# Gated mix of linear and softmax attention: heads four at a time in quarter-array tiles, exponentials over three banks, and an order made by simulation

## The chip, the cores and the metric

One core of a Trainium2 chip. The time is that of one execution on the device, in microseconds (us), median of several; repeats of one kernel in its fast state agree within 0.8% for most kernels here and within 1.4% at the worst (two_banks). A run counts as slow when it is over 1.5% above the fastest of its kernel; times are compared between fast runs only. Engines as the profile names them: PE is the matmul engine (PEld its weight loads), ACT computes the exponentials, DVE does vector work, POOL more vector work, SP issues DMA. PSUM, into which PE writes, is laid out by both kernels as eight banks of 512 f32 values per partition.

Ratios are the mean time of one kernel's fast runs over the mean of the other's fast runs of the same rounds, so they are not quite the ratio of the medians quoted. The experiments ran on several chips; the kernel before took 1294 to 1300 us (medians) beside them, so where two experiments of different calls are compared I use their ratios to it.

## The reference, cut to what matters

```python
x = A_x                                             # 2048 x 512, bf16
g = sigmoid((x * gate_w).sum(-1, keepdims=True))
def A(x):   # linear attention, 32 heads of 16
    q, k, v = split_heads(x @ A_wqkv)
    pq, pk = q @ w_phi[h], k @ w_phi[h]             # 16x16 per head
    phi = lambda p: concat(softmax(p), softmax(-p)) # 32 features
    o = (phi(pq) @ (phi(pk).T @ v)) / (phi(pq) @ phi(pk).sum(seq) + 1e-6)
    return merge_heads(o) @ A_wo
def B(x):   # softmax attention, 32 heads of 16
    q, k, v = split_heads(x @ B_wqkv)
    return merge_heads(softmax(q @ k.T / 4) @ v) @ B_wo
out = g * A(x) + (1 - g) * B(x)
```

Branch B has 32 x 2048 x 2048 exponentials, a million per partition. They set a floor for ACT. PE must deliver the scores in time, with a contraction of only 16 rows (the projections contract over 128).

## The kernel before

All operations carry a guessed time stamp; each engine's instructions are sorted by it and issued in that fixed order. A unit of branch B is two heads, 512 queries and 128 keys: two score matmuls of 64 rows (the other heads' rows of q are zero), one exponential over two banks, two value matmuls.

```python
def add_qk(u, ts_):                       # L436
    for hf in range(2):
        p0 = 64 * hf
        ins = e.matmul(sT[b][:, NQ * hf:NQ * (hf + 1)], lhsT=kT_B[p0:p0 + 64, r, 128 * kt:128 * (kt + 1)],
                       rhs=q64[p0:p0 + 64, m, :], start=True, stop=True, tile_position=(p0, 0))
def add_exp(u, ts_):                      # L447: 128x1024; waits for the value matmuls of three units before
    exp_ops[u] = sch.add("act", ts_, lambda e: e.activation(E_B[:, eb, :], sT[b], ACTF.Exp, scale=SCALE), ...)
def add_pv(u, ts_):                       # L463: 32 columns per head, into one of two accumulators psO
    ...
def add_norm(blk, ts_):                   # 64 blocks of 16 units
    # L480 reciprocal of the whole 64x512 accumulator, L484 clamp,
    # L492 matmul that broadcasts the denominators, L503 copy, L507 product
    op_r = sch.add("dve", tk(t0, 0), lambda e: e.reciprocal(Rb32[p0:p0 + 64, :], psO[par][p0:p0 + 64, :]), ...)
    ...
```

Before the first unit, all k, v and q of branch B (first quarter of queries) are projected. Branch A is threaded between the units; its feature map is a chain PE, DVE (four operations), ACT, DVE (two), POOL.

The softmax here doesn't subtract the row's maximum and nothing guards it: scores larger than these inputs give would overflow.

Of the kernel before, what the change touches and what calls it, by code (L numbers as in the profile page):

```python
# [11 lines left out]

D = 512
H = 32
DH = 16
KT = D // 128
NQ = 512
HP = H // 2
VW = 17
VAW = H * VW + 16  # L20
SCALE = 1.0 / math.sqrt(DH)
SPACING_K = 9.0
SPACING_Q = 45.0
PROJ_STEP = 2.0
EVAC_DELAY = 1.0
STAT_DELAY = 2.0
EPS_TS = 1e-6


class _Op:  # L30
    __slots__ = ("ts", "order", "eng", "fn", "sem", "inc", "waits", "count", "name")

    def __init__(self, ts, order, eng, fn, sem, inc, waits, name):
        self.ts = ts
        self.order = order
        self.eng = eng
        self.fn = fn
        self.sem = sem
        self.inc = inc
        self.waits = waits  # L40
        self.count = None
        self.name = name


class _Sched:
    ENGINES = ("sp", "act", "pe", "dve", "pool")

    def __init__(self):
        self.ops = []
        self.n = 0  # L50
        self.sem_engine = {}

    def add(self, eng, ts, fn, sem=None, waits=(), inc=1, name=""):
        assert eng in self.ENGINES
        ws = []
        for w in waits:
            if w is None:
                continue
            assert isinstance(w, _Op), w
            assert w.ts < ts + 2.5, f"wait on future op: {name}@{ts} waits {w.name}@{w.ts}"  # L60
            assert w.sem is not None, f"producer {w.name} has no semaphore"
            if w.ts >= ts:
                ts = w.ts + EPS_TS
            ws.append(w)
        if sem is not None:
            key = id(sem)
            if key in self.sem_engine:
                assert self.sem_engine[key] == eng, "semaphore incremented by two engines"
            else:
                self.sem_engine[key] = eng  # L70
        op = _Op(ts, self.n, eng, fn, sem, inc, ws, name)
        self.n += 1
        self.ops.append(op)
        return op

    def emit(self, block):
        per_eng = {e: [] for e in self.ENGINES}
        for op in self.ops:
            per_eng[op.eng].append(op)
        for e in self.ENGINES:  # L80
            per_eng[e].sort(key=lambda o: (o.ts, o.order))
        totals = {}
        for e in self.ENGINES:
            for op in per_eng[e]:
                if op.sem is not None:
                    k = id(op.sem)
                    totals[k] = totals.get(k, 0) + op.inc
                    op.count = totals[k]
        starters = {
            "sp": block.sync,  # L90
            "act": block.scalar,
            "pe": block.tensor,
            "dve": block.vector,
            "pool": block.gpsimd,
        }
        for e in self.ENGINES:
            ops = per_eng[e]
            if not ops:
                continue

            def body(engine, ops=ops):
                waited = {}
                for op in ops:
                    for w in op.waits:
                        k = id(w.sem)
                        if waited.get(k, -1) >= w.count:
                            continue
                        engine.wait_ge(w.sem, w.count)
                        waited[k] = w.count
                    ins = op.fn(engine)  # L110
                    if op.sem is not None:
                        assert ins is not None, op.name
                        ins.then_inc(op.sem, op.inc)

            starters[e](body)
# [18 lines left out]
def _build(ctx, nc, A_x, A_wqkv, A_w_phi, A_wo, B_wqkv, B_wo, gate_w, out):  # L134
    S = A_x.shape[1]
    assert A_x.shape[2] == D and S % NQ == 0
    NT = S // 128
    NTQ = NQ // 128
    QC = S // NQ
    KTL = S // 128  # L140
    U = QC * HP * KTL
    TB = 40.0
    _cnt = [0]

    def sb(shape, dt=BF16):
        _cnt[0] += 1
        return ctx.enter_context(nc.sbuf_tensor(f"sbt{_cnt[0]}", shape, dt))

    def tk(base, n):
        return base + n * EPS_TS  # L150

    xT = sb([128, KT, S])
    W_A = sb([128, KT, 3 * D])
    W_B = sb([128, KT, 3 * D])
    Wq64 = sb([128, KT, 16, 128])
    WoA = sb([128, KT, D])
    WoP = sb([128, 8, D])
    Wbd = sb([128, KT, 128])
    kqT_A = sb([128, KT, S])
    vAz = sb([128, NT, 8, 72])  # L160
    kT_B = sb([128, KT, S])

    def ga_ap(i):
        return vAz[:, i, :, :].rearrange("p g c -> p (g c)")[:, 0:D]
    q64 = sb([128, 16, NQ])
    vaug = sb([128, KTL, VAW])
    phi_k = sb([128, 2, 1024])
    phi_q = sb([128, 2, 1024])
    _wbflat = W_B[:].rearrange("p t c -> p (t c)")
    DA = _wbflat[:, 0:2048].rearrange("p (b f) -> p b f", b=2)  # L170
    EA = _wbflat[:, 2048:4096].rearrange("p (b f) -> p b f", b=2)
    statA = sb([128, 2, 3, 64], F32)
    mtmp = sb([128, 3, 64], F32)
    kv_sb = sb([128, 8, 65], F32)
    kzbd = sb([128, 8, 68])
    mask64 = sb([128, 64])
    mask4 = sb([128, 4])
    E_B = sb([128, 3, 1024])
    oTn = sb([128, 2, 8, NQ])
    Rb = sb([128, NQ])  # L180
    Rb32 = sb([128, NQ], F32)
    bcs = sb([128, NQ])
    phi_qT = sb([128, 2, 8, 128])
    oA = sb([128, 2, D])
    oAT = sb([128, 2, KT, 128])
    ident = sb([128, 128])
    sel = sb([128, 64])
    ones = sb([128, 1])
    gw = sb([128, KT])
    g_sb = sb([128, NT], F32)  # L190
    omg = sb([128, NT], F32)
    eg = sb([128, NT], F32)
    fin = sb([128, 2, D])
    denr = sb([128, 2, 32], F32)

    psA = ctx.enter_context(nc.psum_tensor("psA", [128, 2048], F32))
    psO = [ctx.enter_context(nc.psum_tensor(f"psO{i}", [128, 512], F32)) for i in range(2)]
    psM6 = ctx.enter_context(nc.psum_tensor("psM6", [128, 512], F32))
    psM7 = ctx.enter_context(nc.psum_tensor("psM7", [128, 512], F32))
# [3 lines left out]
    s_x = sem("s_x")  # L203
    s_wA = sem("s_wA")
    s_wop = sem("s_wop")
    s_woA = sem("s_woA")
    s_wact = sem("s_wact")
    s_gw = sem("s_gw")
    s_wbd = sem("s_wbd")
    s_out = [sem(f"s_out{i}") for i in range(NT)]  # L210
    s_qk = sem("s_qk")
    s_pv = sem("s_pv")
    s_pe = sem("s_pe")
    s_act = sem("s_act")
    s_dve = sem("s_dve")
    s_pool = sem("s_pool")

    sch = _Sched()
    tasks = []

    def task(ts_, fn):
        tasks.append((ts_, len(tasks), fn))

    op_x = None
    for t in range(KT):
        op_x = sch.add("sp", tk(0.0, t),
                       lambda e, t=t: e.dma_start_transpose(xT[:, t, :], A_x[0, :, t * 128:(t + 1) * 128]),  # L227
                       sem=s_x, inc=16, name=f"dmaxT{t}")
    op_wB = sch.add("act", 0.0, lambda e: e.dma_start(W_B[:], B_wqkv.rearrange("(t p) c -> p t c", p=128)),
                    sem=s_wact, inc=16, name="dmaWB")  # L230
    op_wA = sch.add("sp", 0.1, lambda e: e.dma_start(W_A[:], A_wqkv.rearrange("(t p) c -> p t c", p=128)),
                    sem=s_wA, inc=16, name="dmaWA")
    gwv = gate_w.rearrange("(t p o) -> t p o", p=128, o=1)
    for t in range(KT):
        op_gw = sch.add("pool", tk(0.0, t), lambda e, t=t: e.dma_start(gw[:, t:t + 1], gwv[t]),
                        sem=s_gw, inc=16, name=f"dmagw{t}")

    op_id0 = sch.add("pool", 0.1, lambda e: e.iota(ident[:], [[-1, 128]], channel_multiplier=1,
                                                   allow_small_or_imprecise_dtypes=True), sem=s_pool, name="iota_id")
    op_ident = sch.add("pool", 0.2, lambda e: e.tensor_single_scalar(ident[:], ident[:], 0.0, ALU.is_equal),  # L240
                       sem=s_pool, waits=[op_id0], name="ident")
    op_ones = sch.add("pool", 0.21, lambda e: e.memset(ones[:], 1.0), sem=s_pool, name="ones")
    m64tmp = mtmp[:, 0, :]
    m64tmp2 = mtmp[:, 1, :]
    op_m1 = sch.add("pool", 0.3, lambda e: e.iota(m64tmp.rearrange("p (g c) -> p g c", c=16), [[-32, 4], [0, 16]],
# [49 lines left out]
    for t in range(KT):  # L295
        for j in range(8):
# [5 lines left out]
            op_wbd.append(o)  # L302
    op_wbd_done = op_wbd[-1]

    class Slot:
        def __init__(self, ap):
            self.ap = ap
            self.last_readers = []
# [588 lines left out]
```

## Time and profile before

| | kernel before |
|---|---|
| time, three runs | 1295.46 us (1291.0 to 1299.47) |
| first exponential of branch B | 64.3 us |
| exponentials at their shortest period, added up | 955.0 us |
| everything beyond that between first and last of them | 254.8 us |
| from the start of the last one to the end | 22.1 us |

An exponential's *free period* is the shortest distance from its start to the next one's that repeats: 0.904 us for 128x1024 out of PSUM (0.945 us for the feature maps' 128x1024 out of SBUF). What an interval has above it is called **stall** below. This is better than the mean duration in the profile's groups, which reaches into the next instruction.

The page of the kernel before: busy time, three rows of the forty slices, and costly groups (busy us, mean ns of one, then idle time before them and its releaser).

```profile
PE 1029.4 (79%) x5568; PEld 307.2 (24%) x5568; DVE 639.6 (49%) x773; ACT 995.3 (77%) x1058; POOL 111.1 (9%) x92
...
PE   4999876767698888869687888776878887877775
...
ACT  0077686787777899867698987986989799988993
...
PEclk9989887797889999889799989998999979988998
...
L447 ACT ACTIVATE sbt<-psA 128x1024 bf16<-128x1024 f32 x1024 | 967.6, 1061 | 208.2 <-PE psA L436 205.0
...
L480 DVE RECIPROCAL sbt<-psO 64x512 f32<-64x512 f32 x64 | 214.7, 3355 | 278.7 <-PE psO L463 278.7
```

No engine is full. ACT does the obligatory work and waits 208 us, nearly all for score matmuls (L436). Its first two slices are empty.

Timeline before, in a stretch where PE keeps up (start us, length us, what, idle time before it and its releaser):

```profile
1232.11 0.39 PE L436 MATMUL psA<-sbt 64*128 64x512 bf16 x2 [0.20 <-ACT sbt L447]
...
1232.43 0.39 PE L463 MATMUL psO<-sbt 128*32 128x512 bf16 x2
...
1233.03 0.39 PE L436 MATMUL psA<-sbt 64*128 64x512 bf16 x2 [0.20 <-ACT sbt L447]
...
1233.97 0.40 PE L492 MATMUL psM<-sbt 64*64 64x512 bf16 x1 [0.56 <-DVE sbt L484]
...
1234.30 0.39 PE L463 MATMUL psO<-sbt 128*32 128x512 bf16 x2
```

A score pair starts every 0.92 us, and its value pair follows 0.32 us later: the two matmuls of a pair overlap. The last two lines are the trouble: PE stands before the broadcast matmul L492, which waits for the reciprocal and the clamp, and the value pair behind it in PE's order starts 1.27 us after its score pair in place of 0.32.

### The profile page before, as it was taken

The numbers are of one execution on the slowest core, as the hardware profiler recorded it, in microseconds if no ns is written. First come the engines' busy times: TensorE is split into PE (matmuls) and PEld (weight loads), VectorE is DVE, ScalarE is ACT, GpSimd is POOL, SyncE is SP. The second block draws the span as 40 slices with busy tenths as digits, with TensorE's granted clock in tenths as the row PEclk, the third lists the DMA queues.
The fourth block names the chain that finished last, engine by engine and source line by source line (L and its number), as shares of the span: only waits on it lengthen the run. The fifth ranks groups of instructions, "written<-read, shape, count | busy, mean of one in ns | idle before, by whom it ended". The sixth has DMA issues, their size and how long they took to land.

```text
span 1296.3 us, 14382 instructions
## 1 busy us (share of the span) xinstructions
PE 1029.4 (79%) x5568; PEld 307.2 (24%) x5568; DVE 639.6 (49%) x773; ACT 995.3 (77%) x1058; POOL 111.1 (9%) x92
## 2 busy tenths in 40 slices
PE   4999876767698888869687888776878887877775
PEld 1422221222222222212122222221222222222221
DVE  2734566676655455443544545435445455444332
ACT  0077686787777899867698987986989799988993
POOL 9500011111100000000000000000000000000000
PEclk9989887797889999889799989998999979988998
DMA  6100000000000000000000000000000000000000
GB/s 162 34 1 1 1 1 1 1 1 1 1 1 1 1 1 1 1 1 17 1 1 1 1 1 13 5 1 1 1 1 1 17 1 1 1 1 1 1 1 17
DMA packets 14069, 9.34 MB, mean 7 GB/s; under 512 B 9904, under 2 KB 12976, under 8 KB 14000
## 3 DMA queue, kind: packets, MB, share of 16 engines
q1 hardware_dynamic: 12320, 6.82, 1.9%
q10 hardware_dynamic: 528, 1.57, 0.4%
q8 instruction: 44, 0.72, 0.2%
q14 instruction: 25, 0.20, 0.0%
q0 software_dynamic: 1152, 0.02, 0.0%
HBM read 4.21 MB, written 2.10 MB: 5 GB/s over the span
## 4 chain that ended last, share of the span: by engine, by line
issue 50%; PE 26%; DVE 11%; ACT 8%; POOL 3%; SPq 1%; DMA 0%; ACTq 0%; POOLq 0%; DVEq 0%
PE psA L436 8%; DVE sbt L480 8%; ACT sbt L447 7%; PE psO L463 7%; PE psM L322 6%; POOL sbt L641 3%; PE psA L322 2%; PE psM L523 1%; DVE sbt L484 1%; PE psM L492 1%; SPq L227 1%; PE psM L801 0%; DMA sbt<-in_A_x_dram 0%; PE psM L722 0%; DVE sbt L628 0%
## 5 line engine op out<-in xcount | busy, mean ns | idle before, releaser
L447 ACT ACTIVATE sbt<-psA 128x1024 bf16<-128x1024 f32 x1024 | 967.6, 1061 | 208.2 <-PE psA L436 205.0
L436 PE MATMUL psA<-sbt 64*128 64x512 bf16 x2048 | 426.6, 413 | 124.9 <-ACT sbt L447 115.7
L463 PE MATMUL psO<-sbt 128*32 128x512 bf16 x2048 | 427.6, 414 | 0.7 <-ACT sbt L447 0.7
L480 DVE RECIPROCAL sbt<-psO 64x512 f32<-64x512 f32 x64 | 214.7, 3355 | 278.7 <-PE psO L463 278.7
L436 PEld LDWEIGHTS psA<-sbt 64*128 64x128 bf16 x2048 | 99.2, 94 | 434.5 <-ACT sbt L447 321.8
L322 PE MATMUL psM<-sbt 128*128 128x512 bf16 x448 | 138.0, 441 | 74.1 <-DVE sbt L610 33.5
L463 PEld LDWEIGHTS psO<-sbt 128*32 128x32 bf16 x2048 | 99.5, 94 | 259.3 <-issue 257.8
L641 POOL TENSOR_TENSOR sbt<-sbt 128x1024 bf16<-128x1024 bf16 x32 | 61.7, 1929 | 1078.0 <-DVE sbt L633 1029.9
L326 DVE CAST sbt<-psM 128x512 bf16<-128x512 f32 x90 | 61.8, 687 | 93.9 <-PE psM L322 93.5
L322 PEld LDWEIGHTS psM<-sbt 128*128 128x128 bf16 x448 | 39.5, 105 | 139.0 <-issue 90.8
L503 DVE CAST sbt<-psM 64x512 bf16<-64x512 f32 x64 | 44.0, 687 | 33.2 <-PE psM L492 32.7
L383 ACT ACTIVATE sbt<-psM 128x16 f32<-128x16 f32 x1 | 0.2, 184 | 61.5 <-PE psM L378 61.5
L628 DVE TENSOR_REDUCE sbt<-sbt 128x64 f32<-128x1024 bf16 x32 | 38.8, 1212 | 16.6 <-ACT sbt L619 16.3
L507 DVE TENSOR_TENSOR sbt<-psO,sbt 64x512 bf16<-64x512 f32 x64 | 44.1, 689 | 2.2
L322 PE MATMUL psA<-sbt 128*128 128x512 bf16 x128 | 30.9, 397 | 17.8 <-DMA sbt<-in_A_x_dram 17.8
L492 PE MATMUL psM<-sbt 64*64 64x512 bf16 x64 | 29.1, 455 | 18.3 <-DVE sbt L484 13.3
L619 ACT ACTIVATE sbt<-sbt 128x1024 bf16<-128x1024 bf16 x32 | 35.0, 1095 | 9.1 <-DVE sbt L610 9.1
L598 DVE TENSOR_REDUCE sbt<-psM 128x32 f32<-128x512 f32 x32 | 22.0, 686 | 36.6 <-PE psM L588 30.2
L523 PE MATMUL psM<-sbt 128*128 128x512 bf16 x128 | 31.8, 394 | 4.5 <-DVE sbt L531 3.0
L728 DVE COPY sbt<-psM 128x1024 bf16<-128x1024 bf16 x16 | 11.0, 686 | 35.5 <-PE psM L722 35.3
L531 DVE SCALAR_TENSOR_TENSOR sbt<-psM,sbt 128x512 bf16<-128x512 f32 x16 | 12.0, 750 | 32.5 <-PE psM L523 32.5
L484 DVE TENSOR_SCALAR sbt<-sbt 64x512 bf16<-64x512 f32 x64 | 26.9, 421 | 2.1
(65 smaller groups left out, 365.6 us busy)
## 6 DMA issues: line engine op xcount, KB each, us to landing
out_dram<-sbt SPq DMA_DIRECT2D x16, 128.0 KB, 1.7
sbt<-in_B_wqkv_dram ACTq DMA_DIRECT2D x1, 1536.0 KB, 8.8
sbt<-in_A_wqkv_dram SPq DMA_DIRECT2D x1, 1536.0 KB, 7.6
sbt<-in_B_wo_dram SPq DMA_DIRECT2D x8, 64.0 KB, 2.9
sbt<-in_A_w_phi_dram POOLq DMA_DIRECT2D x32, 0.5 KB, 1.8
sbt<-in_A_wo_dram SPq DMA_DIRECT2D x1, 512.0 KB, 4.3
sbt<-in_A_x_dram SPq DMA_TRANSPOSE x4, 7.6
sbt<-in_gate_w_dram POOLq DMA_DIRECT2D x4, 0.2 KB, 7.4
```

The source lines that it names most:

```text
L322: ins = e.matmul(slot.ap, lhsT=lhsT_list[i], rhs=rhs_list[i], start=(i == 0), stop=(i == n - 1))
L326: evac_fn = lambda e, slot=slot, dst_ap=dst_ap: e.tensor_copy(dst_ap, slot.ap)
L436: ins = e.matmul(sT[b][:, NQ * hf:NQ * (hf + 1)], lhsT=kT_B[p0:p0 + 64, r, 128 * kt:128 * (kt + 1)], rhs=q64[p0:p0 + 64, m, :], start=True ...
L447: exp_ops[u] = sch.add("act", ts_, lambda e: e.activation(E_B[:, eb, :], sT[b], ACTF.Exp, scale=SCALE), sem=s_act, waits=waits, name=f"exp ...
L463: ins = e.matmul(psO[par][c0:c0 + 32, :], lhsT=vaug[:, kt, VW * h: VW * h + 32], rhs=E_B[:, eb, NQ * jb: NQ * (jb + 1)], start=(kt == 0), ...
L480: op_r = sch.add("dve", tk(t0, 0), lambda e: e.reciprocal(Rb32[p0:p0 + 64, :], psO[par][p0:p0 + 64, :]), sem=s_dve, waits=w, name=f"recip{ ...
L484: lambda e: e.tensor_scalar(Rb[p0:p0 + 64, :], Rb32[p0:p0 + 64, :], 1e30, -1e30, op0=ALU.min, op1=ALU.max),
L492: lambda e: e.matmul(psM7[p0:p0 + 64, :], lhsT=sel[p0:p0 + 64, :], rhs=Rb[p0:p0 + 64, :], start=True, stop=True, tile_position=(p0, p0)),
L503: op_cp = sch.add("dve", tk(t0, 1), lambda e: e.tensor_copy(bcs[p0:p0 + 64, :], psM7[p0:p0 + 64, :]), sem=s_dve, waits=wcp, name=f"bccp{blk}")
L507: lambda e: e.tensor_tensor(dst, psO[par][p0:p0 + 64, :], bcs[p0:p0 + 64, :], ALU.mult),
L523: ins = e.matmul(psM7[:], lhsT=oTn[:, qc % 2, j, 128 * i:128 * (i + 1)], rhs=WoP[:, j, :], start=(j == 0), stop=(j == 7))
L641: lambda e: e.tensor_tensor(phi_dst[:, buf, :].rearrange("p (g f) -> p g f", f=DH), EA[:, buf, :].rearrange("p (g f) -> p g f", f=DH), rs. ...
```

## The change

The kernel is rewritten. Its intent:

- q is masked so that a head needs 32 rows; four heads sit in four 32-row tiles of the array. Score tiles are cut in threes, so that an exponential covers three banks (the first 32 still two). Query projections fall from 256 matmuls to 64.
- The accumulator of four heads is copied out by a DVE block transpose, after which the denominators are 16 values per partition: the reciprocal is small, and no broadcast matmul is needed.
- w_phi is multiplied into the projection weights once; gate and 1/denominator are folded together.
- Projections ("fills") are issued one matmul at a time between score and value groups.
- The order comes from a simulation with a duration for each operation; eight exponential buffers replace three.

The diff, cut to its core (the comments are mine; `...` marks cuts):

```diff
-        exp_ops[u] = sch.add("act", ts_, lambda e: e.activation(E_B[:, eb, :], sT[b], ACTF.Exp, scale=SCALE), ...
+        n = 2 if s < 64 else min(3, NTILE - s)
...
+                ins = e.matmul(psS[:, 512 * (base + m):512 * (base + m + 1)],
+                               lhsT=kT_B[32 * i:32 * i + 32, hg // 2, 128 * kt:128 * (kt + 1)],
+                               rhs=qz[32 * i:32 * i + 32, qc % 2, hg, :], start=True, stop=True,
+                               tile_position=(32 * i, 0))
+        op = P.add("pe", 0.30, -100, fn, reads=reads, writes=[("S", j % 2)], name=f"qk{j}")
...
+        op = P.add("act", 0.07 + 0.000833 * 512 * n, 0.0, lambda e: e.activation(
+            Ebuf[:, j % ERING, 0:512 * n], psS[:, 512 * base:512 * (base + n)], ACTF.Exp, scale=SCALE), ...
...
-            op_r = sch.add("dve", tk(t0, 0), lambda e: e.reciprocal(Rb32[p0:p0 + 64, :], psO[par][p0:p0 + 64, :]),
+        P.add("dve", 0.69, -50, lambda e: e.transpose(Tf[:, bb, :], psO[:]), reads=["psO"], ...
+        P.add("dve", 0.15, -40, lambda e: e.reciprocal(rd[:, bb, :], tv[:, :, DH]), reads=[("Tf", bb)], ...
...
+    MM = 0.216                      # simulated duration of one fill matmul
+    def fill(prio, mms, reads, banks=None, name="", chunk=1, dur=MM, after=()):
...
+LAT = 0.12                          # simulated time from one engine's end to another's start,
+MARGIN = 0.35                       # and more where DVE or POOL answers PE or ACT
```

## The prediction

> **What bounds the kernel now.** Span 1296.3 us. The page's busy list gives PE 1029 us (79%), ACT 995 (77%), DVE 640. Neither big engine is full, so I read stages.
> - Up to 63 us (slices, timeline) ACT does nothing: all of k, v, q of the attention branch is projected first; x lands only at 17.8 us.
> - From 63 to 1275 us ACT runs 1024 exponentials of 128x1024. Where PE keeps up (timeline, 500 to 504 and 1230 to 1234 us) one starts every 0.917 us: 939 us, plus 32 feature-map exponentials, about 30 us. The rest is ACT idle: 208 us, 205 of it put down to score matmuls (groups, waits), which stand in PE's fixed order behind a 3.36 us reciprocal (64 of them, 215 us of DVE), projections and feature maps; from 170 to 320 us ACT is at 75% and the granted clock 0.81 to 0.83.
> - Tail: the last exponential is about 21 us before the end.
>
> **What the change does.**
> - Scores come from four 32-row tiles; an exponential covers three banks: 661 of 128x1536, 32 of 128x1024. From 0.917 = 1024 x 0.833 ns + 64 ns I estimate 1.344 us for 1536. The Trainium skill ("ScalarE: Activation LUTs", What ACT_TABLE_LOAD costs) gives 0.833 ns per element plus a fixed part; the period agrees. ACT: 661 x 1.344 + 32 x 0.917 + 32 = about 950 us, only 20 less. The main gain is the 208 us of waiting and 50 us of start.
> - PE: a score pair takes 0.31 to 0.33 us, a value pair the same (timeline, 1234 to 1236 us: 0.645 per unit). Three tiles at once should cost about 0.7 us per 1.344 ("TensorE: Matmul & The Clock Gate", Measured speedup: three column tiles 2.38x; the trace shows only pairs). 694 x 0.7 = 486 us, plus about 180 for 530 full projections and small ones: 670 of 950. Query projections fall from 256 to 64 matmuls.
> - DVE: reciprocals, clamps, casts, products (330 us) become 32 block transposes and small work (50 us); DVE about 290. POOL takes two subtractions per feature map, about 130 us in all.
> - Order: a simulated schedule with eight exponential buffers replaces guessed times, so PE should seldom be stuck before a score matmul.
>
> **Critical path after.** ACT from first to last exponential. First at about 13 us (first quarter of x at 9, projection, copy). Stalls 18 us: 8 in the first head group, which has 84 projection matmuls beside 32 units, 10 around feature maps (whose exponential waits for POOL) and block boundaries. Tail about 9 us: value matmul, transposes, output matmul, store. 13 + 950 + 18 + 9 = **990 us**, range 963 to 1028. Faster by over 2%: 0.97; within 2%: 0.02; slower: 0.01.
>
> **What would show it.** ACT over 93% busy, digits 9 from the second slice; the three-bank exponential at a period near 1.344 us; ACT idle before it under 40 us; PE at most 75%; DVE near 300 us; the chain mostly ACT; first exponential before 15 us.
>
> **What would make it wrong.** Three 32-row tiles not overlapping (score group over 0.6 us): PE bounds, 1100 us or more. PE's granted clock falling to half because PE is less busy, so that the order runs late. ACT stuck behind feature-map exponentials whose POOL inputs are slower than the order assumed (1 us each adds 32). The 24 transposing loads landing later than 9 us.

## The result, and the profile after

| | before | after |
|---|---|---|
| time | 1294.16 us (1291.0 to 1299.47, 4 runs) | 1018.69 us (1017.72 to 1021.52, 4 runs) |
| first exponential of branch B | 64.3 us | 17.4 us |
| free periods added up | 955.0 us | 938.6 us |
| stall | 254.8 us | 49.2 us |
| last one's start to the end | 22.1 us | 10.8 us |
| profiled span | 1296.3 us | 1015.9 us |

The ratio is 0.7867 (95% interval 0.7842 to 0.7892). Of the 280 us between the two profiles, 206 are stall, 47 start, 16 shorter work and 11 tail.

The same parts of the page after:

```profile
PE 864.9 (85%) x5118; PEld 210.8 (21%) x5118; DVE 309.8 (30%) x595; ACT 958.5 (94%) x729; POOL 141.8 (14%) x131
...
PE   7988888878798788788889888888889888888986
...
ACT  3889999998989989999999999999999999999996
...
PEclk8999999997968868955557655555556655555765
...
L512 ACT ACTIVATE E_t<-psS 128x1536 bf16<-128x1536 f32 (+2 forms) x694 | 934.5, 1675 | 33.0 <-PE psS L500 26.4
...
L548 DVE STREAM_TRANSPOSE Tf_t<-psO 128x512 f32<-128x512 f32 x32 | 22.8, 713 | 400.7 <-PE psO L530 400.7
```

ACT is full as predicted, and DVE fell to 310 us. One row was not predicted: the granted PE clock. It is near full up to about 200 us, uneven up to 430 us, and then half of full speed with few exceptions. PE's busy share **rose** to 85% although it does less. By stretch, from the windows view (us, then busy time and instruction count of PE, PEld, DVE, ACT and POOL, then the granted clock, DMA share and GB/s):

```profile
60.00:200.00 140.00, 119.67 (x861) 35.74 (x860) 92.97 (x150) 139.40 (x109) 61.67 (x47) 1.00 0.00 1
200.00:480.00 280.00, 232.54 (x1601) 70.38 (x1598) 148.04 (x308) 261.51 (x197) 66.50 (x50) 0.77 0.01 3
480.00:980.00 500.00, 437.96 (x2292) 85.28 (x2289) 44.85 (x96) 493.50 (x367) 0.00 (x0) 0.55 0.01 3
```

Timeline after, once at full and once at half clock:

```profile
152.15 0.39 PE L500 MATMUL psS<-qz_t,kTB_t 32*128 32x512 bf16 x3
...
152.47 0.40 PE L530 MATMUL psO<-E_t,vaug_t 128*32 128x512 bf16 x3
...
640.59 0.61 PE L500 MATMUL psS<-qz_t,kTB_t 32*128 32x512 bf16 x3 [0.19 <-ACT E_t L512]
...
641.13 0.61 PE L530 MATMUL psO<-E_t,vaug_t 128*32 128x512 bf16 x3
...
641.94 0.61 PE L500 MATMUL psS<-qz_t,kTB_t 32*128 32x512 bf16 x3 [0.19 <-ACT E_t L512]
```

At full clock a value group starts 0.32 us after its score group, as before, although there are now three matmuls in each: quarter tiles do overlap. At half clock it is 0.54 us. Two groups then take 1.08 us of an exponential's 1.344 us, and 0.26 us are left for fills.

The stall by stretch, from the same intervals: 9.1 us up to 100 us, 0.2 us from 100 to 200, 25.6 us from 200 to 450 (branch A's query side), 14.3 us from 450 to the end. The last part comes in lumps, at about 480, 546, 780 and 955 us, while fills (a q projection, then the output projections) run. In between, at half clock, ACT loses nothing to speak of.

### The profile page after: what moved, and what is told of

It reads as the page before. It is cut to its first block, busy times and chain, and to the rows that moved or that the text cites. A ratio compares the mean times of both kernels' runs of the same rounds, so it can differ in the third digit from the quotient of the medians.

```text
span 1015.9 us, 11834 instructions
## 1 busy us (share of the span) xinstructions
PE 864.9 (85%) x5118; PEld 210.8 (21%) x5118; DVE 309.8 (30%) x595; ACT 958.5 (94%) x729; POOL 141.8 (14%) x131
## 4 chain that ended last, share of the span: by engine, by line
ACT 71%; PE 17%; DVE 9%; DMA 1%; issue 1%; SPq 0%; POOL 0%; DVEq 0%
ACT E_t L512 69%; PE psM L435 6%; PE psS L500 4%; PE psO L530 3%; ACT EA_t L670 2%; PE psS L435 1%; DVE oA_t L737 1%; PE psM L712 1%; DVE denr_t L730 1%; DVE stat_t L674 1%; PE psM L719 1%; DVE Pf_t L655 1%; DMA xT_t<-in_A_x_dram 1%; PE psM L739 1%; DVE denr_t L728 1%
## 5 line engine op out<-in xcount | busy, mean ns | idle before, releaser
L512 ACT ACTIVATE E_t<-psS 128x1536 bf16<-128x1536 f32 (+2 forms) x694 | 934.5, 1675 | 33.0 <-PE psS L500 26.4
L500 PE MATMUL psS<-qz_t,kTB_t 32*128 32x512 bf16 x2048 | 363.5, 521 | 98.8 <-ACT E_t L512 95.4
L530 PE MATMUL psO<-E_t,vaug_t 128*32 128x512 bf16 x2048 | 366.7, 526 | 1.2 <-DVE Tf_t L548 0.8
L500 PEld LDWEIGHTS psS<-qz_t,kTB_t 32*128 32x128 bf16 x2048 | 70.8, 96 | 397.3 <-ACT E_t L512 348.4
L530 PEld LDWEIGHTS psO<-E_t,vaug_t 128*32 128x32 bf16 x2048 | 71.3, 99 | 245.2 <-issue 230.8
L435 PE MATMUL psM<-Wp_t,xT_t 128*128 128x512 bf16 x128 | 38.4, 406 | 4.0 <-DVE phiQT_t L715 1.0
L674 DVE TENSOR_REDUCE stat_t<-EA_t 128x64 f32<-128x1024 bf16 x32 | 38.6, 1207 | 5.2 <-ACT EA_t L670 5.0
L435 PE MATMUL psM<-xT_t,WB_t 128*128 128x512 bf16 x112 | 34.6, 418 | 5.7 <-DVE qz_t L464 2.2
L670 ACT ACTIVATE EA_t<-Dd_t 128x1024 bf16<-128x1024 bf16 x32 | 38.4, 1201 | 0.0
L659 DVE TENSOR_REDUCE stat_t<-Pf_t 128x32 f32<-128x512 f32 x32 | 21.7, 679 | 0.9
L661 DVE TENSOR_REDUCE stat_t<-Pf_t 128x32 f32<-128x512 f32 x32 | 21.4, 670 | 0.0
L719 PE MATMUL psM<-kzbd_t,phiQT_t 128*128 128x68 bf16 x128 | 10.9, 216 | 10.9 <-DVE oA_t L737 9.9
```

What stands on the lines that cost most here:

```text
L435: return [lambda e, ap, i=i: e.matmul(ap, lhsT=lhs[i], rhs=rhs[i], start=(i == 0), stop=(i == len(lhs) - 1)) for i in range(len(lhs))]
L500: ins = e.matmul(psS[:, 512 * (base + m):512 * (base + m + 1)], lhsT=kT_B[32 * i:32 * i + 32, hg // 2, 128 * kt:128 * (kt + 1)], rhs=qz[32 ...
L512: op = P.add("act", 0.07 + 0.000833 * 512 * n, 0.0, lambda e: e.activation(Ebuf[:, j % ERING, 0:512 * n], psS[:, 512 * base:512 * (base + ...
L530: ins = e.matmul(psO[32 * i:32 * i + 32, :], lhsT=vaug[:, kt, VW * h:VW * h + 32], rhs=Ebuf[:, j % ERING, 512 * m:512 * (m + 1)], start=(k ...
L670: ex = P.add("act", 0.93, -4, lambda e: e.activation(EA[:, b, :], Dd[:, b, :], ACTF.Exp), reads=[("D", b, 0), ("D", b, 1)], writes=[("EA", ...
L674: P.add("dve", 1.22, prio, lambda e: e.tensor_reduce(stat[:, b, 1, :], e3, AX.X, ALU.add), reads=[("EA", b)], writes=[("ss", b)], name=f"s ...
```

## The experiments

The questions were: is the clock the cause of the remaining stalls (theory A), or does PE stand in its fixed order behind late answers of DVE (theory B); why is the clock low; and what did each part of the change buy?

| run | time, us | ratio | first exponential | stall | tail |
|---|---|---|---|---|---|
| the change | 1018.7 | 0.787 | 17.4 | 49.2 | 10.8 |
| before_copy | 1179.6 | 0.907 | 64.4 | 132.1 | 21.5 |
| before_32rows | 1448.8 | 1.115 | 65.6 | 403.6 | 24.3 |
| two_banks | 1205.3 | 0.928 | 16.2 | 213.9 | 10.9 |
| full_recip | 1030.5 | 0.792 | 16.6 | 60.4 | 14.0 |
| whole_fills | 1037.4 | 0.799 | 18.0 | 69.8 | 10.7 |
| keep_warm | 1012.5 | 0.778 | (slow profile) | | |
| keep_warm_again | 1008.9 | 0.775 | (slow profile) | | |
| start_tail | 1023.3 | 0.788 | 12.7 | 60.4 | 9.4 |
| start_tail_margin | 999.8 | 0.771 | 13.2 | 34.9 | 9.5 |
| margin | 1005.4 | 0.774 | 17.0 | 37.3 | 10.7 |
| late_plain | 995.5 | 0.766 | 13.4 | 39.2 | 9.8 |
| late_junk | 999.7 | 0.771 | 13.2 | 38.7 | 9.7 |

Times are medians of four runs each (for keep_warm the 2091 us run among them); the ratio is to the kernel before. First exponential, stall and tail are of the profiled run.

### before_copy: what the reciprocal cost the kernel before

```diff
-  e.reciprocal(Rb32[p0:p0 + 64, :], psO[par][p0:p0 + 64, :])
+  e.tensor_copy(Rb32[p0:p0 + 64, :], psO[par][p0:p0 + 64, :])
```

> The kernel before, with its 3.36 us reciprocal replaced by a copy of the same shape (0.69 us); wrong result on purpose. Theory: the normalization chain holds the score matmuls of PE in most of the 64 blocks (about 2 us each), so 100 to 150 us of the 242 us of waiting for scores go: 1150 to 1200 us. Rival: the waiting comes from projections and feature maps in PE's order; then at most 40 us go: 1255 us or more.

Measured: 1179.57 us, ratio 0.9068; the result is wrong, as intended. The stall fell from 254.8 to 132.1 us. The waits of ACT in the kernel before and then in this one:

```profile
ACT sbt L447 <- PE psA L436: 205.0, 166, 7.2
```

```profile
ACT sbt L447 <- PE psA L436: 96.1, 140, 6.0
```

The theory's range held (1150 to 1200 us): the length of the reciprocal alone accounted for about half of the waiting of the kernel before. The granted clock rose with it, from 0.91 to 0.95 or more, so a part of the gain may have come by way of the clock. The other half of the waiting is left when that chain is short; it was not split further (the prediction put it down to projections and feature maps in PE's order).

### full_recip: the slow reciprocal put back into the changed kernel

```diff
+        P.add("dve", 3.36, -40, lambda e: e.reciprocal(Tr[:], Tf[:, bb, :]), reads=[("Tf", bb)], writes=["Tr"], ...)
-        P.add("dve", 0.15, -40, lambda e: e.reciprocal(rd[:, bb, :], tv[:, :, DH]), ...)
+        P.add("dve", 0.15, -40, lambda e: e.tensor_copy(rd[:, bb, :], Tr[:].rearrange(...)[:, :, DH]), ...)
-ERING = 8
+ERING = 7
```

> The changed kernel with the full 128x512 reciprocal (3.36 us) back in each of the 32 blocks, after the block transpose has freed the bank (seven exponential buffers in place of eight, for room). Theory: once the accumulator is copied out by the transpose, a slow reciprocal is off the path: plus 3.4 us at the end and 0 to 5 us elsewhere, 1020 to 1030 us. Rival: VectorE being held for 3.4 us delays the drains of PE's fills, and 32 blocks lose 2 us each: about 1080 us.

Measured: 1030.52 us, ratio 0.7921 against 0.7867. This is at the slow edge of the theory's range (1020 to 1030 us) and far from its rival's 1080. The tail grew by 3.2 us, as it must; the stall by 11 us, of which 6.3 us came between 100 and 200 us, where DVE is busy with feature maps; how much of that is the missing eighth buffer and how much DVE being held is not told apart. So the transpose that frees the accumulator first is what took the reciprocal off the path: a reciprocal of the same 3.36 us, 32 times, costs 7 us (by the ratios) to 12 us (by the medians) here, where its 64 copies had cost the old structure about 120.

### two_banks: exponentials over two banks throughout

```diff
-        n = 2 if s < 64 else min(3, NTILE - s)
+        n = 2
```

> The changed kernel with every exponential over two banks (1024 of 128x1024). Theory: ScalarE bounds, so only its fixed part counts: 1024 x 0.917 against 661 x 1.344 + 32 x 0.917 is plus 21 us, that is about 1040 us, with the granted clock higher because PE does the same work per shorter period. Rival: at half clock a score and a value group take 1.08 us, more than 0.917, so that PE bounds wherever the clock is low: 1060 to 1120 us, ScalarE idle over 80 us.

Measured: 1205.28 us, ratio 0.9278. The rival was right, and by more than it said: 187 us slower, not 21. The page of this kernel, then its timeline:

```profile
PE 1157.2 (97%) x5077; PEld 270.8 (23%) x5118; DVE 300.3 (25%) x595; ACT 1054.4 (88%) x1059; POOL 141.9 (12%) x131
...
PEclk9999999689997555555555555555555555555555
...
```

```profile
699.86 0.60 PE L500 MATMUL psS<-qz_t,kTB_t 32*128 32x512 bf16 x2
...
700.39 0.61 PE L530 MATMUL psO<-E_t,vaug_t 128*32 128x512 bf16 x2
...
700.94 0.60 PE L500 MATMUL psS<-qz_t,kTB_t 32*128 32x512 bf16 x2
```

A score and a value group take 1.08 us at half clock whether they hold two tiles or three. Against 0.904 us of ACT that makes PE the bound; against 1.330 us it does not. The third bank pays because it puts half as much exponential work again behind the same PE time, far more than because of the 16 us of fixed cost that it saves ACT.

### before_32rows: one size changed in the kernel before

```diff
-  lhsT=kT_B[p0:p0 + 64, r, 128 * kt:128 * (kt + 1)], rhs=q64[p0:p0 + 64, m, :]
+  lhsT=kT_B[p0:p0 + 32, r, 128 * kt:128 * (kt + 1)], rhs=q64[p0:p0 + 32, m, :]
```

> The kernel before, its score matmuls contracting over 32 rows of the array in place of 64; everything else, order and counts included, is the same (wrong result on purpose: half of the heads are left out). Theory: the granted clock follows how much of the array the matmuls use, and not how busy PE is; so the clock, 0.91 before, falls to about 0.5 in the stretches without projections, groups take 0.54 us each, a unit 1.08 us, and the time rises by 60 to 150 us. Rival: the low clock of the changed kernel comes from PE being idle more of the time (long periods, fewer fills); then clock and time stay at 0.91 and 1300 us.

Measured: 1448.81 us, ratio 1.115; every instruction, its order and its waits are those of the kernel before. (The comparison with the reference still passed, though half of the heads' rows were left out. So it does not see an error in the scores of this size.) The windows of the kernel before, then of this one:

```profile
475.00:945.00 470.00, 377.94 (x2057) 110.11 (x2057) 218.76 (x261) 387.05 (x414) 17.09 (x10) 0.92 0.01 3
1096.00:1282.00 186.00, 141.70 (x784) 39.57 (x782) 78.34 (x84) 164.09 (x176) 3.85 (x2) 0.92 0.00 1
```

```profile
475.00:945.00 470.00, 428.24 (x1834) 106.13 (x1833) 194.45 (x232) 359.88 (x367) 15.41 (x8) 0.65 0.01 3
1096.00:1282.00 186.00, 175.51 (x750) 43.15 (x748) 80.58 (x97) 149.54 (x153) 7.71 (x4) 0.62 0.01 3
```

Half as many rows per score matmul, nothing else in the program, and the granted clock falls from 0.92 to 0.62, while PE is busy for more of the time (its matmuls take longer at the lower clock). So the clock did not fall because PE was idle. (The data change with the rows: the heads left out now give scores of zero. That this moved the clock is not excluded here, but in the changed kernel no head is left out, and its clock is low too.) In the changed kernel PE never stood idle for more than 0.63 us between 480 and 1005 us, at a clock of about 0.55; in the kernel before it stood idle for up to 3.4 us between 1096 and 1279 us and kept 0.92. In these runs what counts is how much of the array a matmul uses; by which measure exactly, they do not say.

The Trainium skill ("TensorE: Matmul & The Clock Gate", What's actually happening) says that the clock is set "based on how busy the PE has been recently", and its section "Why this matters for your kernels" advises against PE-idle gaps of over about 3 us. The two levels that it gives, half and full, agree with the clock records of these traces, which hold only 0.5 and 1.0; a granted clock between them is a mean over time. The advice about gaps does not suffice: PE with no gap above 0.63 us, in narrow tiles, was held at half for most of the time.

### keep_warm and keep_warm_again: buying the clock back

```diff
+            for _ in range(junk):        # 1 from the 141st score group on
+                e.matmul(psS[:, 512 * base:512 * base + 512], lhsT=kT_B[:, 0, 0:128], rhs=kT_B[:, 0, 0:512],
+                         start=True, stop=True)
-        op = P.add("pe", 0.30, -100, fn, ...)
+        op = P.add("pe", 0.30 + 0.3 * junk, -100, fn, ...)
```

> The changed kernel, with one throw-away full-array matmul (128x512) ahead of every score group from the 141st on; it is overwritten by the scores, so the result stays right. Theory A (clock): most of the about 40 us of exponential stalls after 200 us come from the granted clock falling to 0.5, which makes score and value groups 0.54 us each where the order assumed 0.30. The added matmul lifts the granted clock after 200 us to 0.9 or more, the stalls after 200 us fall from about 40 us to under 15, and the time to about 990 to 1000 us (from 1019). Theory B (order): PE stands still because VectorE answers late in the feature-map chain, and the low clock is only its consequence; then the clock rises but the time stays within 1010 to 1022 us. Theory C: the low clock is free since ScalarE bounds; same as B.

> The same kernel as keep_warm, for a profile of the fast state. If the 2091 us execution was a passing state of that chip, none of these is slow: 1008 to 1016 us, granted clock about 0.96. If the added matmuls provoke it, it comes again. In the fast profile the exponential stalls after 200 us should be about 10 us less than in the changed kernel: what is left must be PE in its order behind VectorE.

Measured: 1012.54 us with a granted clock of 0.94 to 0.96 in the three fast runs, and 1008.9 us with 0.96 to 0.975. The clock did come back, but only 11 to 15 us of time with it (by the ratios, 0.7781 and 0.7751 against 0.7867), between what theory A and theory B expected. The reason shows in the timeline of keep_warm_again. Its profile is slow (1022 us), so only its mechanism is used. First where the clock held, then where it had been lost:

```profile
600.09 0.39 PE L505 MATMUL psS<-qz_t,kTB_t 32*128 32x512 bf16 x3
...
601.11 0.39 PE L501 MATMUL psS<-kTB_t 128*128 128x512 bf16 x1 [0.30 <-ACT E_t L517]
...
601.43 0.39 PE L505 MATMUL psS<-qz_t,kTB_t 32*128 32x512 bf16 x3
...
903.80 0.61 PE L505 MATMUL psS<-qz_t,kTB_t 32*128 32x512 bf16 x3
...
904.46 1.45 ACT L517 ACTIVATE E_t<-psS 128x1536 bf16<-128x1536 f32 x1 [0.18 <-PE psS L505]
...
904.89 0.61 PE L501 MATMUL psS<-kTB_t 128*128 128x512 bf16 x1
...
905.43 0.61 PE L505 MATMUL psS<-qz_t,kTB_t 32*128 32x512 bf16 x3
```

At full clock the added matmul is free: a score group every 1.34 us. At half clock the three pieces take 1.63 us, ACT waits 0.18 us each time, and it goes on for 72 us, until the clock is back. No fill runs in that time: the clock returns at 952.2 us, just after a block boundary at which two added matmuls came without a value group between them, and fills start only at 952.9 us; what brought it back is not shown. (In the changed kernel it came back within a batch of full-array fills: 543.7 to 548.8 us, clock full from 548.3 us.) The remedy makes the bad state worse.

One of the eight executions of this kernel took 2091 us, with no clock record at all (which is printed as a granted clock of 1.0) and every 512-column matmul or group at about 0.83 us, from the warming matmuls at the very start, before the first added one:

```profile
901.39 0.91 PE L501 MATMUL psS<-kTB_t 128*128 128x512 bf16 x1
...
902.23 0.91 PE L505 MATMUL psS<-qz_t,kTB_t 32*128 32x512 bf16 x3
```

That is about a quarter of full speed (at full clock each further matmul of a fill adds 0.22 us: the timeline after has three in 0.82 us and four in 1.04). The Trainium skill's page "TensorE: Matmul & The Clock Gate", in "Seeing it yourself", warns that the clock has been seen stuck at a quarter for over 50 us and that its records are unreliable; here it held for a whole execution. It came once, and no explanation is offered; that run is left out of all comparisons.

### margin: only the order's assumptions

```diff
+BANKLAT = 0.45
-  bs = [b for b in op.acq.banks if b.free and b.shared]
+  bs = [b for b in op.acq.banks if b.free and b.shared and all(o.end + BANKLAT <= t + 1e-9 for o in b.last)]
             if prev is None:
                 op.acq = f
+                op.margin = 1.0
```

> The changed kernel with only the order's assumptions changed (0.45 us before a drained bank is refilled, 1.0 us before a fill reads what another engine wrote); no added matmuls. If late VectorE answers ahead of PE are the larger cause, the exponential stalls after 200 us fall from about 37 us to under 25 us although the clock stays at 0.5 after 450 us, and the time to 1003 to 1012 us (the start, crammed with fills, may lose 3 to 5 us, as in start_tail_margin). If the half clock is the larger cause, 1016 us or more.

Measured: 1005.39 us, ratio 0.7740 against 0.7867. The stall from 200 to 450 us fell from 25.6 to 14.8 us, with the clock there hardly changed (0.81 for 0.77, between 200 and 480 us); after 450 us it fell only from 14.3 to 12.1 us. So theory B holds for about 11 us of the query-side stretch. The window of this run, to be held against the changed kernel's 0.77:

```profile
200.00:480.00 280.00, 234.06 (x1662) 73.19 (x1662) 167.24 (x332) 268.98 (x206) 78.90 (x59) 0.81 0.01 3
```

Raising the clock there did less, and less surely: with the added matmuls and the old order the stall from 200 to 450 us was 16.1 us in keep_warm_again (slow profile) and 23.8 us in start_tail, at a clock of 0.96 and 0.93; with both remedies it was 15.7 us (start_tail_margin), no less than with the margins alone. This is how it goes in the changed kernel at 225 us (DVE and POOL, then PE and ACT):

```profile
225.74 1.93 POOL L678 TENSOR_TENSOR phiQ_t<-EA_t,stat_t 128x1024 bf16<-128x1024 bf16 x1 [1.26 <-DVE stat_t L676]
225.81 1.89 DVE L730 TENSOR_SCALAR denr_t<-denr_t,g_t 128x16 f32<-128x16 f32 x1
...
228.21 0.61 PE L739 MATMUL psM<-ident_t,oA_t 128*128 128x128 bf16 x4 [1.51 <-DVE oA_t L737]
...
228.75 0.61 PE L500 MATMUL psS<-qz_t,kTB_t 32*128 32x512 bf16 x3
...
229.41 1.45 ACT L512 ACTIVATE E_t<-psS 128x1536 bf16<-128x1536 f32 x1 [0.29 <-PE psS L500]
...
231.89 1.89 PE L435 MATMUL psM<-Wp_t,xT_t 128*128 128x512 bf16 x4
...
233.71 0.61 PE L500 MATMUL psS<-qz_t,kTB_t 32*128 32x512 bf16 x3
...
234.37 1.45 ACT L512 ACTIVATE E_t<-psS 128x1536 bf16<-128x1536 f32 x1 [1.46 <-PE psS L500]
```

A DVE product of 16 columns, 0.235 us as a rule and 0.1 us in the simulation, took 1.89 us while a POOL product of 1.93 us ran. It happened to 3 of 32 (1.89, 1.54 and 1.48 us), and in a small way to 3 more (0.30 to 0.50 us). PE stood for 1.51 us in front of the transposes that wait for it, the clock is half by then, and the fill of four matmuls at 231.89 us, which the order had put into a gap with 0.216 us each, took 1.8 us and held the scores. The two theories are links of one chain here. That POOL's product held the small one back was not tested by a run of its own, but the traces leave little doubt: the two lines above end 0.03 us apart (227.67 and 227.70), and so it is with each of the 34 lengthened products in the five traces looked at (this one, margin, keep_warm_again, start_tail_margin, late_plain): whenever it began, it ended 0.03 us after a POOL operation. It agrees with the skill ("GPSIMD Engine Reference", Specifications), which lists POOL's SBUF interfaces as shared with the vector engine, with contention for DVE instructions that have two SBUF inputs or run in a 2-port mode; in which mode this product ran, no record here shows.

### whole_fills: projections in one piece

```diff
-    def fill(prio, mms, reads, banks=None, name="", chunk=1, dur=MM, after=()):
+    def fill(prio, mms, reads, banks=None, name="", chunk=8, dur=MM, after=()):
```

> The changed kernel with each projection's four to eight matmuls in one uninterrupted piece (as the kernel before issues them) in place of single ones between score and value groups. Theory: a piece of four takes 0.9 us at full and 1.7 us at half clock, against 0.7 us of slack per exponential, so it delays scores: plus 20 to 50 us. Rival: eight exponential buffers hide it, within 8 us of 1019.

Measured: 1037.39 us, ratio 0.7988: 16 us by the ratios (0.0121 of about 1298 us), a little under the stated range of the theory and clearly more than its rival allowed. The stall rose from 49.2 to 69.8 us. Eight exponential buffers do not hide it. The likely reason, read from the kernel and not tested, is that the scarce buffers are the two sets of score banks ahead of ACT.

### start_tail, start_tail_margin, late_plain, late_junk: towards a better kernel

start_tail is keep_warm with a shorter start and end:

```diff
-    for i, (nm, o) in enumerate((("wbk", D), ("wbq", 0), ("wbv", 2 * D))):
+    for i, (nm, o) in enumerate((("wbk", D), ("wbq", 0))):       # wbv moved to SP, after the first quarter of x
-        for _ in range(14):                                      # warming matmuls
+        for _ in range(28):
-            f, mm = fill(30 + c, proj([gwb[:, t, :] for t in range(KT)],
+            f, mm = fill(42 + c, proj([gwb[:, t, :] for t in range(KT)],
-              reads=[("pre", i)], writes=[("fin", tile % 2)], ...
+              reads=[("pre", i)], writes=[("phiQ", i // 2), ("last", i)], ...   # a buffer for each of the last stores
```

> keep_warm, and a shorter start and end: the value weights load after the first quarter of x, 28 warming matmuls in place of 14, the gate after the first head group, the last four stores from buffers of their own. Expected against keep_warm (1009 us): first exponential at about 13.5 us in place of 17, 3 us fewer stalls before 65 us, tail 2 to 3 us shorter: about 1001 us. If the start is bound by the transposing loads alone, only the tail moves: 1006 us.

> start_tail, and an order that assumes 0.45 us before a drained bank can be refilled and 1.0 us before a fill can read what VectorE or GpSimd wrote. Theory B (PE stands behind late VectorE answers in its fixed order): stalls of the exponential after 200 us fall by 10 us or more, to about 990 us. Rival: the stalls come from sheer PE load in that stretch; then within 4 us of start_tail.

> margin with the two assumptions used only after 60 us, and the start and tail of start_tail; no added matmuls. Against the changed kernel: start minus 5 us and minus 4 us of early stalls, tail minus 1 us, stalls minus 10 us: about 998 us. At half clock the outputs of each quarter still cost 2 to 3 us each.

> late_plain with one throw-away matmul per score group in the feature-map stretch only (slots 140 to 350, about 200 to 480 us), so that the clock is kept where fills are dense, and no added matmul can make PE the bound when the clock falls later. Expected 5 to 10 us under late_plain: about 990 us. If the added matmuls only displace fills, equal to late_plain.

start_tail missed: 1023.25 us. Its first exponential is at 12.7 us for 17.4, as expected, and the stall up to 100 us is 6.5 us for 9.1; but later it lost the clock with the added matmul in place (a granted clock of 0.86 between 450 and 700 us), and the stall after 450 us is 26.7 us for the changed kernel's 14.3, which took back the gain. The shorter start is seen in the first projections of the changed kernel and of start_tail:

```profile
12.30 3.57 PE L435 MATMUL psS<-xT_t,WB_t 128*128 128x512 bf16 x8 [5.75 <-DMA xT_t<-in_A_x_dram]
```

```profile
9.01 1.89 PE L438 MATMUL psS<-xT_t,WB_t 128*128 128x512 bf16 x8
```

The first quarter of x had landed at 12.2 us, sharing the DMA with 1.5 MB of weights, and the 14 warming matmuls had ended 5.75 us earlier, so the first eight projections ran at half clock.

start_tail_margin, with margin's assumptions as well, took 999.84 us. The improvement on start_tail, about 23 us, is over twice the 10 us that were expected as the least; it contains luck with the clock (0.99 from 450 us on), so it is not all the order's doing. Its stall after 450 us is 7.9 us, against 12.1 us in margin at half clock: the nearest that these runs come to the price of the half clock there. late_plain, without added matmuls and with the new assumptions only after 60 us, took 995.52 us (990.74 to 1002.78), ratio 0.7656 (0.7611 to 0.7701) against the change's 0.7867: it beats both kernels. That is as expected (998 us), but not in its parts: its profiled run, the slowest of the four, has 15.0 us of stall before 100 us, where 4 us fewer than the changed kernel's 9.1 were expected, and 13.4 us after 450 us at half clock. late_junk, which adds the throw-away matmuls only in the query-side stretch, took 999.74 us (ratio 0.7711, interval 0.7663 to 0.7759): not the 5 to 10 us below late_plain that were expected, and the two intervals overlap (the other case of the expectation: no gain where the added matmuls only displace fills). Its profile shows a single wait of 10.4 us, for a score group that needs the next quarter's q. The order had put that query projection behind the other fills, which had less room beside the added matmuls (DVE's copies of q, then PE and ACT):

```profile
338.15 1.54 DVE L471 TENSOR_SCALAR qz_t<-psM,pmask_t 128x512 bf16<-128x512 f32 x2 [1.98 <-PE psM L442]
...
339.50 0.61 PE L511 MATMUL psS<-qz_t,kTB_t 32*128 32x512 bf16 x3
...
340.15 4.15 ACT L523 ACTIVATE E_t<-psS 128x1536 bf16<-128x1536 f32 x3 [10.43 <-PE psS L511]
```

So the added matmuls were not tested fairly there. That giving the query projections precedence would bring late_junk below late_plain is argued, not run.

## Why the prediction was right or wrong

**Time: 990 us predicted, range 963 to 1028; 1018.7 us measured.** Inside the range, near its slow end. The terms of the sum against the profile (13 + 950 + 18 + 9 predicted):

- *"First at about 13 us (first quarter of x at 9, projection, copy)"*: 17.4 us. x landed at 12.2 us; the prediction took no account of 1.5 MB of weights on the same DMA engines, nor of a cold clock for the first projections. start_tail shows both: 12.7 us once they are mended.
- *Work, "about 950 us"*: with the free periods it is 938.6 us. The estimate of 1.344 us per three-bank exponential contained 14 ns of hand-over between PE and ACT, some 9 us over 661 of them; but most follow at 1.330 us, about a quarter at 1.340 to 1.345 us, and all these hand-overs add up to only 1.4 us. The mechanism is right, the size 11 us too large.
- *"Stalls 18 us"*: 49.2 us above the free periods. This term was the one mis-sized, by about 30 us, of which the 11 us too many in the work term made up a third: that the sum stayed near is in part luck. The prediction gave 8 us to the first head group, where 9 us are seen up to 100 us, and 10 us to feature maps and block boundaries. What it lacked was the query side of branch A at a varying clock (25.6 us) and the later fills at half clock (14.3 us).
- *Tail, 9 us*: 9.8 us from the end of the last exponential.

**The bound and the mechanism: right.** ACT is 94% busy, DVE 310 us, quarter tiles overlap, and most of the gain (206 of 280 us) is waiting that went. before_copy confirms the reading that the reciprocal chain was a large part: about 120 of 255 us of stall.

**"PE at most 75%": wrong**, 85%. The groups cost 0.64 us per exponential at full clock, under the estimated 0.7, but 1.08 us at half.

**"Only 20 less. The main gain is ...": wrong in what it implies.** On ACT the three banks do save about 16 us. But the prediction costed them for ACT alone. two_banks shows that without them the kernel takes 1205 us: they keep PE, slowed at the low clock that came with its narrow tiles, below ACT. The parts of the change can't be priced one by one: 32-row tiles put alone into the kernel before, two at a time, were a loss of 150 us (before_32rows).

**"PE's granted clock falling to half because PE is less busy, so that the order runs late"**: listed as a danger, and it came, with the wrong reason. before_32rows shows the clock falling while PE is more busy. And it costs less than feared for most of the run, since 1.08 us fits into 1.344 us; it costs where fills must fit into the remaining 0.26 us. The prediction had not worked out whether the groups still fit at half clock; that they do, in three banks and not in two, was luck.

**"ACT stuck behind feature-map exponentials whose POOL inputs are slower"**: did not happen; POOL's subtractions took 1.06 us, within the 1.1 us that the order assumed, and the releasers of ACT's waits in the profile are score and value groups. POOL did harm in another way, beside DVE's small products.

**Open:** what exactly the activity measure counts; how the last 40 us of stall split between clock and order, since each brings the other about; the one execution at a quarter of the clock.

## What to carry to other kernels

Narrow matmuls packed side by side in the array took the time of one here (three in 0.32 us), but they can cost the granted clock: read the clock by stretch, and check that the groups at **half** speed still fit below the bounding engine's period, with room for what else PE must do. Price a wider exponential by the ratio of PE time to ACT time per instruction, not by its fixed cost alone. In a fixed order, give the simulated durations of the clock that the stretch will really have (advice that no run here tested; margin changed only the waits) and allow for late answers where POOL and DVE work side by side; filler matmuls to hold the clock are free only while they work, and when the clock is lost they deepen the loss.

## What the Trainium skill lacked or had wrong

- "TensorE: Matmul & The Clock Gate", What's actually happening and Why this matters for your kernels: the clock is explained by how busy PE is and guarded by avoiding gaps. Lacking: narrow tiles count for less. Score matmuls of 32 rows for 64, nothing else changed, took the granted clock from 0.92 to 0.62 (1096 to 1282 us) and the time from 1299 to 1449 us; the changed kernel sat near 0.55 for 500 us with no PE idle time above 0.63 us.
- The same page, Measured speedup vs the span model, and "TensorEngine Tiling (Array Packing)", Theoretical Speedup: the gains of packing are given without the loss of clock. Three 32-row tiles took 0.32 us from score to value group at full clock, the same as a pair of 64-row tiles, and 0.54 us at the half clock that they led to.
- The same page, Seeing it yourself: a clock stuck at a quarter is told of for over 50 us. One execution of eight of one kernel stayed there for all its 2089 us, with no clock record (0.83 us per 512 columns).
- "ScalarE: Activation LUTs", What ACT_TABLE_LOAD costs: 186 ns + 0.833 ns per element with an overlap of 93 ns back to back (its formula for immediate operands) would be 0.946 and 1.373 us for 1024 and 1536 elements. For the feature maps' exponential out of SBUF (bf16, always followed by one out of PSUM) the free period is 0.945 us, which agrees; out of PSUM (f32) it is 0.904 and 1.330 us, a fixed part of about 50 ns. This section gives no separate figure for PSUM; the skill as a whole is not silent on it.
